# Products with V on four of the eight 64x32 tiles of TensorE, a head in two halves of 1024 queries with one accumulator bank

## The chip, the cores and the metric

The kernel runs on one core of a Trainium2 chip. A core has TensorE (matrix products; its results go to PSUM, eight banks of 128 partitions x 512 float32), VectorE, ScalarE and GpSimd for everything else, and DMA queues for transfers. The metric is the device time of one execution in microseconds (us). The profile names the engines PE (TensorE's products), PEld (its weight loads), DVE (VectorE), ACT (ScalarE), POOL (GpSimd) and SP (the queue that issues most transfers).

## The reference

Two multi-head attentions over the same x, mixed token by token with a gate (cut to what matters):

```python
x = A_x                                   # 1 x 2048 x 512, 32 heads of 16
g = sigmoid((x * gate_w).sum(-1, keepdims=True))
# for each of A and B, with its own wqkv and wo:
qkv = (x @ wqkv).reshape(B, S, 3, H, Dh)  # q, k, v
scores = einsum("bhqd,bhkd->bhqk", q, k) * Dh ** -0.5
p = softmax(scores, axis=-1)
o = einsum("bhqk,bhkd->bhqd", p, v)
a_or_b = o.reshape(B, S, D) @ wo
return g * a + (1 - g) * b
```

All data is float32. So there are 64 heads in all, each with 2048 x 2048 scores.

## The kernel before

**Stages.** A prologue splits the inputs into high and low parts, computes q, k and v for all heads (products of 128x128 weights with 512 columns, L298 and L351) and stores them to memory. Then one long loop runs over 1024 *rounds*: a round is one tile of 128 keys of one head, 16 rounds to a head. Finished heads are stored unnormalised with their denominators (17 rows: 16 of the head and one of sums), and read back, normalised and multiplied with wo some heads later (`project_out`, L564): side 0 after head 31, in four groups of four output tiles, side 1 after head 55, the last group in the tail.

**A round.** TensorE is used as eight independent tiles of 64 rows x 32 columns: two row halves (rows 0 to 63 and 64 to 127, `HALVES`) times four column groups. Three kinds of work run on them:

- *Scores* (`score`, L218): for 128 keys and 512 queries, four products of 50 rows x 32 columns, on the four tiles of one row half; the two halves take turns (`rows()`). One PSUM bank `ps_st` per 512 queries. ScalarE turns it into exponentials (L220, the letter `e`), which go to a buffer `p` of 2048 queries.
- *Maxima* for a head that comes 22 rounds later (`max_plain`, L153, letter `m`): the same shape with queries as rows, into a bank `ps_m`, reduced by VectorE (L159). One bank of each two rounds goes another way: ScalarE first writes a relu of a small difference product (`max_rise`, L166, letter `D`, bank `ps_st`), and VectorE reduces bank and relu together (`max_pair`, L171, letter `A`).
- *Products with V* (`attend`, L697): for each 128 queries ("a quarter" of 512) the 128 keys as two halves of 64, each on its own row half and into its own accumulator bank (`acc[0]`, `acc[1]`); the four chunks of 512 queries lie on the four column groups. All eight tiles work on it. The operands are float32.

**The order** is written out by hand. For two rounds it is one of two equal strings

```python
FULL = "Dmemme3eem2emmeeAe3", "Dmemme3eem2emmeeAe3"
```

where a digit issues that many quarters for all four chunks. Each engine takes its instructions in this order. The products with V run two rounds behind the exponentials. PSUM: three banks `ps_m`, three `ps_st`, two accumulators.

**End of a head** (L716 to L723): ScalarE copies both accumulators to SBUF (L720, two copies), GpSimd adds them (L722), and a transfer stores the head (`od`). The first product with V of the next head must wait for these copies, since it overwrites the accumulators. Before it come six banks of scores in the order (`D m e m m e`).

**The last 22 rounds** have no more maxima to compute: the order is `LATE`, and all six free banks take scores in turn (`ring`, `result_bank`). The last head runs its queries in four blocks of 512, so that its outputs can be normalised and projected one block at a time (`tail`, `add_parts`, `token_gates`).

**In the prologue** the v projections (`project_v`, L351, one `ps_st` bank each) alternate with `run_ahead`: after every second one, six banks of scores for the maxima of the first heads, of which every second lies in a `ps_st` bank too (`early`).

## Time and profile before

| what | us |
|---|---|
| median of 3 runs (lowest, highest) | 2723.86 (2723.26, 2723.9) |
| the profiled execution's own time | 2724.57 |
| its span | 2722.8 |
| busy PE / PEld / DVE / ACT / POOL | 2577.0 / 1521.8 / 2361.3 / 2401.3 / 355.4 |
| granted TensorE clock, mean | 0.999 |

The page of the profile gives, for each group of instructions, the line of the kernel, the engine, the operation, output and inputs with their shapes, how many there were, the busy time, the mean length in nanoseconds of one record, and the idle time of the engine just ahead of them with what ended it. Records of one engine overlap, because its pipeline takes the next instruction before the last has ended; so the mean length of one is longer than the time from one to the next. A float32 product with V has two records (the page lists 32320 for about 16160 instructions). The rows by window give each engine's busy time and, in brackets, its number of instructions.

### The profile page before, as it was taken

How to read it: one execution, taken by the hardware profiler on the slowest of the kernel's cores; microseconds unless marked ns; L12 is line 12 of the kernel's file. 1: busy time of each engine (PE TensorE's matmuls, PEld its weight loads, DVE VectorE, ACT ScalarE, POOL GpSimd, SP SyncE). 2: the span in 40 equal slices, each digit the busy share in tenths (PEclk: the TensorE clock that was granted, in tenths of full speed). 3: DMA queues.
4: the chain of work that ended last, by engine and by line, in shares of the span. 5: the costliest groups of instructions: out<-in, count | busy, mean ns of one | idle time of the engine just before them, and what ended most of it. 6: DMA issues, size and time to landing. Idle time of an engine off the chain costs nothing.

```text
span 2722.8 us, 147771 instructions
## 1 busy us (share of the span) xinstructions
PE 2577.0 (95%) x66710; PEld 1521.8 (56%) x66710; DVE 2361.3 (87%) x4474; ACT 2401.3 (88%) x4862; POOL 355.4 (13%) x594
## 2 busy tenths in 40 slices
PE   9999999999999999999999999999999999999998
PEld 7777555555555555555555565555555555555553
DVE  5444799999999999999999978899999999998884
ACT  4222699999999999999999968899999999998796
POOL 2010022220000000000100323000100011012212
PEclk9999999999999999999999999999999999999999
DMA  5342212111111111111211322111111111112102
GB/s 199 113 159 99 71 47 66 54 51 39 51 38 32 34 42 51 38 40 39 62 36 34 100 61 75 35 33 33 54 38 39 40 58 46 32 57 84 44 25 96
DMA packets 95934, 159.62 MB, mean 59 GB/s; under 512 B 26182, under 2 KB 43974, under 8 KB 95302
## 3 DMA queue, kind: packets, MB, share of 16 engines
q1 hardware_dynamic: 91590, 139.68, 16.4%
q8 instruction: 522, 8.55, 1.4%
q0 software_dynamic: 2560, 8.91, 1.3%
q10 hardware_dynamic: 1152, 1.57, 0.2%
q14 instruction: 110, 0.90, 0.1%
HBM read 100.56 MB, written 49.54 MB: 55 GB/s over the span
## 4 chain that ended last, share of the span: by engine, by line
PE 73%; ACT 17%; DVE 7%; issue 2%; DMA 1%; SPq 0%; DVEq 0%; ACTq 0%
PE acc L697 30%; PE ps_st L218 20%; ACT p L220 15%; PE ps_m L153 9%; PE ps_st L298 6%; DVE mxp L159 6%; PE ps_st L351 3%; PE ps_m L564 3%; ACT ev L720 2%; PE ps_st L153 1%; DVE rise L171 1%; DMA x_st<-xd 0%; DVE rn L520 0%; DMA raw<-in_xT 0%; PE ps_st L564 0%
## 5 line engine op out<-in xcount | busy, mean ns | idle before, releaser
L220 ACT ACTIVATE p<-ps_st 128x512 f32<-128x512 f32 x4044 | 2105.1, 725 | 82.3 <-PE ps_st L218 77.8
L159 DVE TENSOR_REDUCE mxp<-ps_m 128x1 f32<-128x512 f32 x3048 | 1893.0, 682 | 160.5 <-PE ps_m L153 64.8
L218 PE MATMUL ps_st<-q_st,k_st 50*32 50x512 f16 x16192 | 1516.7, 382 | 82.8 <-ACT p L220 0.5
L697 PE MATMUL acc<-p,vg 64*17 64x384 f32 (+1 forms) x32320 | 1367.6, 379 | 39.3 <-ACT ev L720 35.5
L153 PE MATMUL ps_m<-k_st,q_st 48*32 48x512 f16 x14192 | 1118.7, 380 | 1.7 <-DVE mxp L171 1.3
L218 PEld LDWEIGHTS <-k_st 50*32 50x32 f16 x16384 | 636.8, 89 | 834.4 <-issue 712.9
L697 PEld LDWEIGHTS acc<-p,vg 64*17 64x17 f32 x32320 | 553.7, 92 | 117.6 <-ACT ev L720 54.4
L153 PEld LDWEIGHTS <-q_st 48*32 48x32 f16 x16384 | 444.1, 89 | 145.8 <-issue 57.0
L166 ACT ACTIVATE rise<-ps_st 128x512 f32<-128x512 f32 x500 | 357.2, 715 | 0.0
L171 DVE CUSTOM_DVE_ANT_0 rise<-ps_m,rise 128x512 f32<-128x512 f32 x500 | 340.6, 681 | 0.0
L722 POOL TENSOR_TENSOR ev<-ev_lo,ev 128x512 f32<-128x512 f32 x63 | 80.4, 1277 | 1022.5 <-ACT ev L720 1022.5
L153 PE MATMUL ps_st<-x_st,q_st 48*32 48x512 f16 x2000 | 210.4, 377 | 0.0
L181 POOL TENSOR_SCALAR mrow<-mrow 128x16 f32<-128x16 f32 x64 | 16.4, 257 | 1018.5 <-DVE mrow L180 1018.5
L318 ACT ACTIVATE parts<-ps_st 128x512 f16<-128x512 f32 x64 | 38.0, 597 | 111.8 <-PE ps_st L298 105.1
L319 DVE SCALAR_TENSOR_TENSOR parts<-ps_st,parts 128x512 f16<-128x512 f32 x64 | 44.0, 691 | 95.8 <-ACT parts L318 89.7
L354 ACT COPY v_st<-ps_st 128x512 f32<-128x512 f32 x32 | 18.8, 587 | 98.9 <-PE ps_st L351 96.5
L564 PE MATMUL ps_m<-wo,ot 128*128 128x512 f32 x348 | 83.7, 395 | 2.2 <-DVE mxp L159 2.2
L564 PEld LDWEIGHTS ps_m<-wo,ot 128*128 128x128 f32 x348 | 64.7, 189 | 21.3 <-issue 5.5
L298 PE MATMUL ps_st<-xh,whi 128*128 128x512 f32 x224 | 59.9, 389 | 0.0
L298 PE MATMUL ps_st<-xh,wlo 128*128 128x512 f32 x224 | 59.9, 389 | 0.0
L298 PE MATMUL ps_st<-xl,whi 128*128 128x512 f32 x224 | 59.9, 389 | 0.0
L298 PEld LDWEIGHTS ps_st<-xh,wlo 128*128 128x128 f32 x224 | 42.0, 188 | 8.8
(120 smaller groups left out, 997.2 us busy)
## 6 DMA issues: line engine op xcount, KB each, us to landing
k_st<-kd SPq DMA_DIRECT2D x128, 128.0 KB
q_st<-qd SPq DMA_DIRECT2D x128, 128.0 KB
od<-ev SPq DMA_DIRECT2D x63, 256.0 KB
vd<-v_st SPq DMA_DIRECT2D x32, 272.0 KB
vg<-vd POOLq DMA_DIRECT2D x32, 272.0 KB, 4.2
qd<-parts SPq DMA_DIRECT2D x32, 256.0 KB
kd<-parts SPq DMA_DIRECT2D x32, 256.0 KB
k_st<-kd SPq DMA_DIRECT2D x128, 64.0 KB
```

The source lines that it names most:

```text
L153: pe.matmul(ps[j:j + 32], q[b:b + SC, t * P + j:t * P + j + 32], k, start=True, stop=True, tile_position=(b, j))
L159: dve.tensor_reduce(o[:, c:c + 1], ps, op=ALU.max, axis=AX.X)
L166: act.activation(rises[m], ps, AF.Relu)
L171: dve.tensor_tensor_reduce(out=rise, in0=ps, in1=rise, scale=1.0, scalar=LOWEST, op0=ALU.add, op1=ALU.max, accum_out=o[:, 0:1])
L218: pe.matmul(ps[j:j + 32], k[b:b + SC + 2, kk * P + j:kk * P + j + 32], q[b:b + SC + 2, cc * 512:(cc + 1) * 512], start=True, stop=True, ti ...
L220: act.activation(pt[r][:, c * 512:(c + 1) * 512], ps, AF.Exp, scale=SCALE / UNIT ** 2)
L298: pe.matmul(ps, w[a][:, k], (xh, xl)[b][cc][:, k], start=n == 0, stop=n == 3 * KC - 1)
L351: pe.matmul(ps, a[:, k, o:o + P], b[:, k], start=n == 0, stop=n == 3 * KC - 1)
L564: pe.matmul(ps, ot[a][:, slot, tt * P:(tt + 1) * P], wt[b][:, g], start=first and i == 0, stop=last and i == 2)
L697: pe.matmul(acc[i][32 * c:32 * c + 17, qa * P:qb * P], v[b:b + 64, 4 * a + c if final else kt, j], p[b:b + 64, c * 512 + qa * P:c * 512 + ...
L720: act.copy(parts[i], acc[i])
L722: pool.tensor_tensor(ev, parts[0], ev, op=ALU.add)
```

## The change

- **Tiles.** `tiles_of(0)` is rows 0 to 63 with columns 0 to 63 and rows 64 to 127 with columns 64 to 127; `tiles_of(1)` is the other four tiles. All products with V run on the first four. A bank of scores goes to whichever four have less work issued to them (`load`, one unit for a quarter or a bank), so mostly to the second. Every bank of scores is now written half from one row half and half from the other.
- **One accumulator.** The two key halves of a product now lie in different partitions of one bank: keys 0 to 63 in partitions 0 to 63 and keys 64 to 127 in partitions 64 to 127, for two chunks of 512 queries. So a bank holds 1024 queries, and a head runs in two halves: all 16 key tiles for queries 0 to 1023, then all for 1024 to 2047. A *unit* is one key tile and 1024 queries, two to a round. The freed bank goes to `ps_st` (four instead of three).
- **End of a half head.** One copy of the one bank: by VectorE for the first half (both halves of head 62 and the last head's first three blocks too), by ScalarE for the second; then the store. The two key halves are no longer added by GpSimd at once; they are stored apart and added when they are read back (`add_den`, `add_num`, on GpSimd, one add for the denominators of a group and one for each group and chunk). The stores, and the loads of numerators and denominators, are twice as many or more.
- **Order.** `FULL` covers four rounds; the quarters are spread as one or two at a time between the banks of scores. A digit issues quarters of one unit, four instructions each. The end of every half head falls on the end of the string, with six banks of scores (`m e A D e m`) between the last product with V of the old half and the first of the new one. The row work of VectorE is called at the letters `Q` and `R`.
- One `max_rise` moves from the end of the prologue into the loop.

At the end of a head, ScalarE's order changes. The names are the exponentials (`p<-ps_st`), the relu (`rise`) and the copies out of the accumulators; before:

```order
L166 ACTIVATE rise<-ps_st 128x512
L220 ACTIVATE p<-ps_st 128x512 x8
L720 COPY ev_lo<-acc_74 128x512
L720 COPY ev<-acc_75 128x512
L166 ACTIVATE rise<-ps_st 128x512
L220 ACTIVATE p<-ps_st 128x512 x8
```

and now, at the end of a second half:

```order
L165 ACTIVATE rise<-ps_st 128x512
L222 ACTIVATE p<-ps_st 128x512 x9
L743 COPY ev<-acc 128x512
L222 ACTIVATE p<-ps_st 128x512
L165 ACTIVATE rise<-ps_st 128x512
L222 ACTIVATE p<-ps_st 128x512 x6
```

Two copies for each head have become one; the exponentials and relus are as many as before.

The other copy is in VectorE's order, at the end of a first half, between the reductions (`mxp<-ps_m`; the two ISA rows are the one of L170):

```order
L158 TENSOR_REDUCE mxp<-ps_m 128x1 x6
L743 COPY ev<-acc 128x512
L158 TENSOR_REDUCE mxp<-ps_m 128x1
L170 ISA rise,mxp<-ps_m,rise 128x512
L170 ISA mxp 128x1
L179 TENSOR_REDUCE mrow<-mxp 128x16
```

where before there were only reductions at this point:

```order
L159 TENSOR_REDUCE mxp<-ps_m 128x1 x6
L171 ISA rise,mxp<-ps_m,rise 128x512
L171 ISA mxp 128x1
L159 TENSOR_REDUCE mxp<-ps_m 128x1 x3
L180 TENSOR_REDUCE mrow<-mxp 128x16
```

VectorE gets one more operation for each head.

The diff, cut to its core (what is left out are the layouts of the loads and stores, the last head's schedule and the end of the prologue):

```diff
-    ps_st = ctx.enter_context(tc.tile_pool(name="ps_st", bufs=3, space=PSUM))
+    ps_st = ctx.enter_context(tc.tile_pool(name="ps_st", bufs=4, space=PSUM))
...
-    acc = [ps_acc.tile([P, 512], F32, name=f"acc{i}") for i in range(2)]
+    acc = ps_acc.tile([P, 512], F32, name="acc")
...
+    load = [0, 0]
+
+    def tiles_of(i):
+        return [(HALVES[(j // 64 + i) % 2], j) for j in range(0, P, 32)]
+
+    def next_tiles():
+        i = int(load[0] >= load[1])
+        load[i] += 1
+        return tiles_of(i)
...
-        for j in range(0, P, 32):
-            pe.matmul(ps[j:j + 32], q[b:b + SC, t * P + j:t * P + j + 32], k, start=True, stop=True,
+        for b, j in next_tiles():
+            pe.matmul(ps[j:j + 32], q[b:b + SC, t * P + j:t * P + j + 32], k[b:b + SC], start=True, stop=True,
                       tile_position=(b, j))
...
-        for j in range(0, P, 32):
+        for b, j in next_tiles():
             pe.matmul(ps[j:j + 32], k[b:b + SC + 2, kk * P + j:kk * P + j + 32],
                       q[b:b + SC + 2, cc * 512:(cc + 1) * 512], start=True, stop=True, tile_position=(b, j))
...
+    def add_num(G, c):
+        pool.tensor_tensor(nums[G, c], nums[G, c], nums.pop(("p", G, c)), op=ALU.add)
...
+    def attend(u, qa, qb):
+        h, w = divmod(u, 2 * NT)
...
+        for i, (b, d) in enumerate(tiles_of(0)):
+            c = i % 2
+            pe.matmul(acc[d:d + 17, qa * P:qb * P], v[b:b + 64, 2 * (w % n) + c if h == NH - 1 else w % n, j],
+                      pt[u][b:b + 64, c * 512 + qa * P:c * 512 + qb * P], start=w % n == qa == 0,
+                      stop=w % n == n - 1, tile_position=(b, d), skip_group_check=True)
+        load[0] += qb - qa
...
-            parts = [work.tile([P, 512], F32, name=n) for n in ("ev_lo", "ev")]
-            for i in range(2):
-                act.copy(parts[i], acc[i])
-            ev = parts[1]
-            pool.tensor_tensor(ev, parts[0], ev, op=ALU.add)
-            nc.sync.dma_start(od[G][j].rearrange("c r t -> (c r) t"), ev)
+            ev = work.tile([P, 512], F32, name="ev")
+            (dve.tensor_copy if w < NT or h == NH - 2 else act.copy)(ev, acc)
+            nc.sync.dma_start(od[G][j, w // NT].rearrange("c r t -> (c r) t"), ev)
...
-    FULL = "Dmemme3eem2emmeeAe3", "Dmemme3eem2emmeeAe3"
-    EDGE = FULL
-    LATE = "ee4eeee4ee"
+    FULL = "QDQemQ2e1m1e2em1Qe1m2eQ1Dm1e2AQ1em1e3mem1e1Q2e1m1e1m1e1m1e1RQ2mReA"
+    LATE = "e2" * 8
...
                 for a in projects:
                     project_out(*a)
+                    load[:] = [0, 0]
                 projects.clear()
```

## The prediction

> **What bounds the kernel now.** I read the page's chain first, then busy time by window, then the groups and waits of the long loop, then the timeline at the places that the change touches. The chain alone misleads:

> ```profile
> PE 73%; ACT 17%; DVE 7%; issue 2%; DMA 1%; SPq 0%; DVEq 0%; ACTq 0%
> ```

> PE's records carry a modelled, pipelined end, so they nearly always touch. The windows (busy PE, PEld, DVE, ACT, POOL; instructions in brackets) say more. They are the prologue, the loop, the side 0 projections, the loop, the side 1 projections and the last head:

> ```profile
> 60.00:310.00 250.00, 239.54 (x1512) 180.38 (x1515) 108.14 (x171) 62.41 (x109) 25.16 (x28) 1.00 0.34 117
> 600.00:1500.00 900.00, 852.81 (x25422) 482.08 (x25414) 862.98 (x1660) 899.54 (x1836) 69.53 (x153) 1.00 0.15 41
> 1515.00:1707.00 192.00, 182.87 (x4552) 110.91 (x4552) 160.25 (x300) 157.62 (x322) 60.44 (x75) 1.00 0.23 72
> 1720.00:1912.00 192.00, 182.05 (x5420) 102.92 (x5419) 183.94 (x354) 191.91 (x392) 10.04 (x25) 1.00 0.13 38
> 2395.00:2585.00 190.00, 180.81 (x4742) 107.25 (x4728) 166.53 (x316) 163.57 (x334) 40.34 (x53) 1.00 0.20 62
> 2667.00:2705.00 38.00, 34.93 (x485) 13.29 (x486) 16.34 (x33) 30.96 (x63) 13.43 (x18) 0.96 0.21 75
> ```

> In the loop ACT is busy 899.54 of 900 us with 1836 instructions: 0.490 us each, end to end. A head is 64 exponentials, 8 relus and 2 copies, 74 x 0.490 = 36.26 us. DVE is busy 95.9%, idle 37 us in 24.8 heads, 1.49 us a head. The groups (whole run), and the loop's waits:

> ```profile
> L220 ACT ACTIVATE p<-ps_st 128x512 f32<-128x512 f32 x4044 | 2105.1, 725 | 82.3 <-PE ps_st L218 77.8 <-PE ps_m L218 3.5
> L218 PE MATMUL ps_st<-q_st,k_st 50*32 50x512 f16 x16192 | 1516.7, 382 | 82.8 <-ACT p L220 0.5 <-ACT v_st L354 0.2
> L697 PE MATMUL acc<-p,vg 64*17 64x384 f32 x15968 | 1004.7, 484 | 35.5 <-ACT ev L720 35.5
> L697 PE MATMUL acc<-p,vg 64*17 64x128 f32 x15968 | 332.9, 269 | 0.0
> L579 DVE TENSOR_SCALAR o_acc<-ps_m,gate 128x512 f32<-128x512 f32 x16 | 12.0, 751 | 31.5 <-PE ps_m L564 31.5
> L520 DVE RECIPROCAL rn<-dn 128x32 f32<-128x32 f32 x28 | 9.7, 345 | 0.0
> ```
> ```profile
> PEld L218 <- issue: 276.1, 870, 0.5
> PEld acc L697 <- ACT ev L720: 20.9, 24, 0.9
> ```

> PE's weight loads for the scores stand still 276.1 us in these 900: PE is ahead and waits for a bank that ACT has not read. So ACT is the bound in the loop, DVE is next, and PE has about 30% to spare. In the projection windows ACT is busy only 82% and 86%: PE starves it.

> **The copies: the term that should be certain.** The end of one head, in the timeline (start, length, what):

> ```profile
> 631.25 0.64 ACT L720 COPY ev_lo<-acc 128x512 f32<-128x512 f32 x1
> 631.72 0.67 ACT L720 COPY ev<-acc 128x512 f32<-128x512 f32 x1
> 632.20 0.69 ACT L166 ACTIVATE rise<-ps_st 128x512 f32<-128x512 f32 x1
> 632.44 0.87 PE L697 MATMUL acc<-p,vg 64*17 64x384 f32 x16 [0.57 <-ACT ev L720]
> ```

> From one copy to the next is 0.48 us. Heads 0 to 61 lose one of two: 62 x 0.48 = **-29.8**. Head 62 loses both: **-1.0**.

> The copy on DVE has no row before. Below, it costs a reduction of the same 512 columns, 0.60 from one to the next (below, at 283); above, the 0.751 of L579, which writes 512 columns from PSUM. I take 0.60. It hides in DVE's 1.49 us of idle time, which falls to 1.49 - 0.60 - 0.48 = 0.41 a head. That cover is thin; without it, what exceeds 0.41 comes back on the path (second rival). Queued behind the copy on DVE are one to three reductions, and PE waits for their banks; ACT meanwhile has e, D, e, 3 x 0.49 = 1.5 us, besides what is queued.

> PE now waits at the accumulator twice a head instead of once (20.9/24 = 0.87 us). Below: one copy less, 0.4 each. Above: a copy behind three reductions, 4 x 0.60 = 2.4. Either is covered by 276.1/24.8 = 11 us of waiting for ACT. Cost 0.

> **PE's own work.** From 128 to 384 columns a record grows by 215 ns, so 128 columns take 107 ns in each of two records, 0.215 us a quarter; the rest, 0.16, is pipeline. A score bank is 382 - 162 = 220 ns. Before, a tile has 64 quarters and 64 banks a head: 13.8 + 14.1 = 27.9 us of 36.26. Now one four have 128 quarters, 27.5 us, and the other four up to 128 banks, 28.2, of 35.78. The sum is unchanged; cost 0. Pieces of 128 columns already run at full rate:

> ```profile
> 1001.24 0.66 PE L697 MATMUL acc<-p,vg 64*17 64x128 f32 x32
> ```

> 32 records on eight tiles, four deep: (0.66 - 0.16)/4 = 0.125 us each, the stagger of eight starts included.

> **The fourth `ps_st` bank, in the prologue.** One pair of v projections with its six score banks:

> ```profile
> 282.74 0.40 PE L153 MATMUL ps_st<-k_st,q_st 48*32 48x512 f16 x4
> 283.01 0.68 DVE L159 TENSOR_REDUCE mxp<-ps_st 128x1 f32<-128x512 f32 x1
> 283.61 0.68 DVE L159 TENSOR_REDUCE mxp<-ps_m 128x1 f32<-128x512 f32 x1
> 283.75 0.76 PEld L351 LDWEIGHTS ps_st<-wvhi,xh 128*128 128x128 f32 x4 [0.91 <-DVE mxp L159]
> 283.75 1.20 PE L351 MATMUL ps_st<-wvhi,xh 128*128 128x512 f32 x4 [0.61 <-DVE mxp L159]
> ```

> A pair takes five `ps_st` banks: projection, three of the six scores, projection. With three, the second projection needs the bank of the first such score and waits for its reduction, the second one (283.01 + 0.68 = 283.69; it starts at 283.75). With four it takes the first projection's bank, which ACT has emptied. In the prologue's waits:

> ```profile
> PEld ps_st L351 <- DVE mxp L159: 14.4, 16, 0.9
> PE ps_st L351 <- DVE mxp L159: 9.7, 16, 0.7
> ```

> PE bounds this stage (239.54 of 250), DVE works only 108, so nothing is late next. Bounds -9.7 (products) and -14.4 (weight loads); the product's record ends 0.16 after its tile is free, which makes up most of the difference: **-14.4**.

> **Projections.** Eight times (four for each side) PE runs several output tiles in a row and ACT starves:

> ```profile
> 1562.78 11.14 PE L564 MATMUL ps_m<-wo,ot 128*128 128x512 f32 x48 [0.28 <-DVE mxp L159]
> 1573.85 0.86 PE L697 MATMUL acc<-p,vg 64*17 64x384 f32 x16
> 1574.51 0.42 PE L218 MATMUL ps_st<-q_st,k_st 50*32 50x512 f16 x8
> 1574.96 2.56 ACT L220 ACTIVATE p<-ps_st 128x512 f32<-128x512 f32 x5 [11.44 <-PE ps_st L218]
> ```

> The first exponential's scores wait 0.66 us behind products with V that hold all eight tiles. Now these hold four; the scores wait for one bank of maxima, 0.22: -0.44. A fourth bank lets ACT work up to 0.49 longer into the burst: 0 to -0.49. Per burst -0.4 to -0.9, times 8 = -3.5 to -7.4. PE is far ahead there, so the fourth bank is full: **-7.3**. GpSimd's adds (16 a side, about 1.3 us each) fit beside its 60 of 192 us.

> **Losses.** At each of seven group ends DVE makes four reciprocals of 0.345 us, 1.4 us. They hid in 1.49 a head; now in 0.41: 0 to 1.0 each; **+3** of 0 to 7.

> In the last 22 rounds ACT needs 8 x 0.49 = 3.92 us for two rounds. PE needed 8 x 0.215 + 4 x 0.22 = 2.6; now the first four tiles alone need 16 x 0.215 = 3.4. The output projections of the last head, some 9 us on all tiles, had 8 x 1.3 = 10.7 us to fit into and now have 8 x 0.5 = 3.9: up to +5, though ACT already loses 38 - 30.96 = 7 us there. The last products with V run on four tiles, 8 x 0.215 = +1.7. Against it, on the chain at the end

> ```profile
> 2708.46 0.54 issue
> 2709.00 0.68 DVE o_num L551
> 2709.68 0.61 DVE ev L708
> 2710.32 0.63 ACT ev_hi L710
> ```

> ACT now makes `ev_hi` straight from the accumulator, which takes out the add (0.61) and some of what it waited for: about -1.3. Together -2 to +7: **+3**.

> More stores and loads (window share of DMA 0.15) and GpSimd's loss of 63 adds of 1.3 us lie off the path. The store now waits for one copy, not copy and add, so what is behind it on SP (the next head's loads) is not later.

> **Sum.** 2724.6 (the profiled execution, 1.8 over its span) - 29.8 - 1.0 - 14.4 - 7.3 + 3 + 3 = 2678; the median of the runs lies 0.7 below that execution: **2677 us**, 1.7% faster.

> **The rivals.**

> *DVE takes over (chance 0.13).* If the copy and the hitch of PE waiting behind it cost 0.5 us a head more than DVE's 0.41, ACT's gain is gone: the head stays 36.3, and the prologue and the projections remain: 2724 - 14 - 7 + 3 = 2706. For it: 98.9% busy. Against: the 1.49 is the records' figure, in which every pause hides 0.08 (681 ns a record, 600 from one to the next); the true slack is larger.

> *PE becomes the bound (0.09, slower).* Its place is the chain of quarters on the first four tiles: 128 a head must each take less than 36.26/128 = 0.283 us to be faster than before, against 0.215. If each of the two passes showed 40 ns more, because a four-tile queue hides the weight load (92 ns a record) less than eight did, a quarter would take 0.295, a head 37.8, and the time 2724 + 62 x 1.5 - 14 = 2803. Against: the 0.125 us of the 32-record row.

> *The two row halves exclude each other in a bank (0.02, slower).* Before, each score bank and each accumulator was written from one row half. Now all are written from both. If these took turns, a quarter would take 0.43, a head 55 us, the time about 3900. [...]

> **Chances and range.** Forecast 0.74, rivals 0.13, 0.09, 0.02, the rest small shifts. Its own range: all losses at their worst and the smaller gains, 2724 - 31 - 10 - 3.5 + 7 + 7 = 2694; the other way, 2724 - 31 - 14 - 7 - 2, with up to 8 more if the smoother order ends small waits, 2662. The DVE rival widens it: 2660 to 2708. What can be told from no change here is 0.2%, 5 us. Faster 0.87, same 0.03, slower 0.10.

> **What would show it.** Right: in the loop ACT still above 99% with 73 instructions a head, heads of 35.8 us; no L351 wait for DVE; ACT's pauses at the bursts near 10.5 instead of 11.44; DVE near 98%. Wrong: waits of ACT for `ps_st` in the loop, PE's 276 us of waiting gone, or the products with V longer than 0.215 us a quarter.

## The result, and the profile after

The changed kernel takes 2854.61 us (median of 4 runs, 2852.75 to 2859.02), the kernel before 2723.65 on the same chip: ratio 1.0483, 95% interval 1.0465 to 1.0501. It is **slower by 131 us** where 47 us less were predicted. The profiled execution took 2855.93, its span is 2854.1.

The windows of the changed kernel, to be held against those of the kernel before (busy PE, PEld, DVE, ACT, POOL):

```profile
60.00:310.00 250.00, 247.02 (x2092) 190.36 (x2091) 122.51 (x198) 77.47 (x139) 25.98 (x32) 1.00 0.35 122
600.00:1500.00 900.00, 806.02 (x30189) 579.93 (x30172) 837.49 (x1601) 864.47 (x1723) 40.77 (x131) 1.00 0.16 47
1515.00:1707.00 192.00, 168.53 (x5391) 122.65 (x5378) 153.46 (x289) 151.49 (x303) 55.98 (x66) 0.97 0.27 89
1720.00:1912.00 192.00, 178.85 (x5729) 126.31 (x5717) 162.42 (x311) 159.80 (x322) 20.27 (x37) 0.99 0.15 44
```

In the loop ACT is busy 96.1% instead of 99.9%, and DVE less than before too. PE is *less* busy (806 of 900 us, before 853) although it got through *more* instructions: 30189 + 30172 in 900 us, 67.0 a microsecond, where before 25422 + 25414 were 56.5. So nothing on DVE, ACT or PE's array is full. The waits of the same 900 us say who stands still:

```profile
PEld L152 <- issue: 93.2, 251, 1.8
PEld acc L720 <- issue: 86.8, 124, 1.5
PE acc L720 <- issue: 46.5, 93, 1.2
PEld L220 <- issue: 38.6, 90, 1.2
DVE mxp L158 <- PE ps_m L152: 36.9, 91, 1.1
ACT p L222 <- PE ps_st L220: 24.3, 63, 1.1
```

"issue" is time in which the engine waited for nothing that the profile shows. Before, such a pause of PE lasted at most 0.5 us and stood at the scores and the maxima (`PEld L218`, and 19.8 us at L153), where the prediction read it as PE waiting for a bank. Now it lasts up to 1.8 us and stands in front of products with V as well, and DVE and ACT wait for PE. The chain of waits has 9% "issue" where it had 2%:

```profile
PE 68%; DVE 14%; issue 9%; ACT 5%; DMA 3%; SPq 1%; POOL 0%; ACTq 0%; DVEq 0%; POOLq 0%
```

In the timeline the pauses come at a beat. Three neighbours (start, length, what, and the idle time ahead of it):

```profile
1000.14 0.29 PE L720 MATMUL acc<-p,vg 64*17 64x128 f32 x3 [0.70 <-issue]
1003.88 0.29 PE L720 MATMUL acc<-p,vg 64*17 64x128 f32 x3 [0.31 <-issue]
1007.63 0.40 PE L720 MATMUL acc<-p,vg 64*17 64x128 f32 x4 [0.47 <-issue]
```

They are 3.74 and 3.75 us apart. In the records of these 900 us, 242 of PE's instructions (weight loads included) start over 0.35 us after the one before, and half of these lie exactly 256 instructions apart (123 of 241 spacings; in `v_128`, a run told of below, 171 of 207). The page's first row and its list of DMA queues give the reason away; of the changed kernel:

```profile
PE 2589.7 (91%) x83094; PEld 1856.0 (65%) x83094; DVE 2405.9 (84%) x4538; ACT 2414.3 (85%) x4794; POOL 325.3 (11%) x583
q8 instruction: 650, 10.65, 1.6%
```

and of the kernel before:

```profile
q8 instruction: 522, 8.55, 1.4%
```

10.65 MB in 650 packets are 16384 bytes each. They are 64 bytes for each of the 2 x 83094 PE instructions, and the same division gives 64 before (2 x 66710). So q8 carries PE's instructions, 256 to a packet. This gives a theory, called F below: **PE is fed its instructions in blocks of 256, and no faster than one block in about 3.75 us.** A head of the changed kernel has 2560 of them: `FULL` has 24 pieces of V for four rounds, 96 a head, each four instructions on each of four tiles, 1536, and the 128 banks of scores and maxima have 8 each, 1024. (The trace has 2558 a head. The expectations below say 2608, which is a miscount.) That is ten blocks, 37.5 us at 3.75, and the heads took 38.3. A head before had 2048, 8 blocks, 30 us, which fitted into ACT's 36.26.

Where the 131 us lie, by the ends of every 64th exponential on ACT (us; the three right columns are runs that are told of below):

| stretch | before | after | v_512 | v_512_add | v_512_add_dve |
|---|---|---|---|---|---|
| to the first exponential of the loop's head 0 | 287.9 | 273.8 | 274.0 | 272.6 | 273.9 |
| head 0 | 49.5 | 48.9 | 46.2 | 46.2 | 46.2 |
| heads 1 to 32 | 1161.7 | 1225.7 | 1159.9 | 1159.9 | 1149.4 |
| heads 33 to 37 (projections, side 0) | 227.7 | 253.4 | 253.0 | 226.6 | 225.2 |
| heads 38 to 56 | 689.5 | 721.6 | 688.0 | 688.0 | 682.3 |
| heads 57 to 61 (projections, side 1) | 213.7 | 234.7 | 218.1 | 212.5 | 210.6 |
| heads 62 and 63 | 74.8 | 75.8 | 77.6 | 74.3 | 77.4 |
| behind the last exponential | 17.9 | 20.1 | 20.2 | 20.2 | 20.2 |
| span | 2722.8 | 2854.1 | 2737.1 | 2700.2 | 2685.1 |

The prologue's gain is there. Of the other stretches head 0 is 0.6 us shorter than before, and all the rest are longer.

### The profile page after: what moved, and what is told of

Read it like the earlier page. It is cut to its first block, busy times and chain, and to the rows that moved or that the text cites. A ratio compares the mean times of both kernels' runs of the same rounds, so it can differ in the third digit from the quotient of the medians.

```text
span 2854.1 us, 181748 instructions
## 1 busy us (share of the span) xinstructions
PE 2589.7 (91%) x83094; PEld 1856.0 (65%) x83094; DVE 2405.9 (84%) x4538; ACT 2414.3 (85%) x4794; POOL 325.3 (11%) x583
## 3 DMA queue, kind: packets, MB, share of 16 engines
q8 instruction: 650, 10.65, 1.6%
q0 software_dynamic: 2560, 8.91, 1.1%
## 4 chain that ended last, share of the span: by engine, by line
PE 68%; DVE 14%; issue 9%; ACT 5%; DMA 3%; SPq 1%; POOL 0%; ACTq 0%; DVEq 0%; POOLq 0%
PE acc L720 30%; PE ps_st L220 13%; PE ps_m L152 12%; DVE mxp L158 10%; PE ps_st L300 6%; ACT p L222 4%; PE ps_st L353 3%; PE ps_m L587 3%; DVE rise L170 2%; PE ps_st L152 2%; DMA o_part<-od 1%; DVE ev L743 1%; ACT ev L743 1%; ACT rise L165 1%; DMA q_st<-qd 0%
## 5 line engine op out<-in xcount | busy, mean ns | idle before, releaser
L222 ACT ACTIVATE p<-ps_st 128x512 f32<-128x512 f32 x4051 | 2146.5, 675 | 208.7 <-PE ps_m L152 104.5
L720 PE MATMUL acc<-p,vg 64*17 64x128 f32 (+2 forms) x48672 | 2066.3, 308 | 157.7 <-issue 139.9
L158 DVE TENSOR_REDUCE mxp<-ps_m 128x1 f32<-128x512 f32 x3048 | 1920.8, 682 | 208.0 <-PE ps_m L152 130.6
L220 PE MATMUL ps_st<-q_st,k_st 50*32 50x512 f16 x16220 | 1640.6, 381 | 46.8 <-issue 36.0
L720 PEld LDWEIGHTS acc<-p,vg 64*17 64x17 f32 x48672 | 1325.1, 93 | 385.0 <-issue 238.0
L152 PE MATMUL ps_m<-k_st,q_st 48*32 48x512 f16 x14192 | 1486.4, 381 | 42.7 <-issue 30.2
L152 PEld LDWEIGHTS <-q_st 48*32 48x32 f16 x16384 | 584.1, 90 | 317.0 <-issue 212.3
L220 PEld LDWEIGHTS <-k_st 50*32 50x32 f16 x16384 | 582.7, 90 | 205.9 <-issue 129.5
L170 DVE CUSTOM_DVE_ANT_0 rise<-ps_m,rise 128x512 f32<-128x512 f32 x500 | 341.6, 683 | 29.9 <-PE ps_m L152 14.3
L165 ACT ACTIVATE rise<-ps_st 128x512 f32<-128x512 f32 x500 | 337.0, 674 | 5.6 <-PE ps_st L152 4.8
L152 PE MATMUL ps_st<-x_st,q_st 48*32 48x512 f16 x2000 | 210.6, 380 | 4.0 <-issue 2.7
L180 POOL TENSOR_SCALAR mrow<-mrow 128x16 f32<-128x16 f32 x64 | 16.5, 257 | 1724.9 <-DVE mrow L179 1724.9
L559 POOL TENSOR_TENSOR o_num<-o_num,o_part 128x512 f32<-128x512 f32 x32 | 40.8, 1276 | 234.2 <-DMA o_part<-od 234.2
```

Source lines behind the costliest of these rows:

```text
L152: pe.matmul(ps[j:j + 32], q[b:b + SC, t * P + j:t * P + j + 32], k[b:b + SC], start=True, stop=True, tile_position=(b, j))
L158: dve.tensor_reduce(o[:, c:c + 1], ps, op=ALU.max, axis=AX.X)
L165: act.activation(rises[m], ps, AF.Relu)
L170: dve.tensor_tensor_reduce(out=rise, in0=ps, in1=rise, scale=1.0, scalar=LOWEST, op0=ALU.add, op1=ALU.max, accum_out=o[:, 0:1])
L220: pe.matmul(ps[j:j + 32], k[b:b + SC + 2, kk * P + j:kk * P + j + 32], q[b:b + SC + 2, cc * 512:(cc + 1) * 512], start=True, stop=True, ti ...
L222: act.activation(pt[u][:, c * 512:(c + 1) * 512], ps, AF.Exp, scale=SCALE / UNIT ** 2)
```

## The experiments

### The number of instructions, and nothing else

F says that the count alone matters, whatever tiles, banks or copies. Two kernels have the same count, 3072 a head, and share little else: `v_128` is the changed kernel with its products with V cut into four pieces of 128 columns at eight places of the order, and `before_128` is the kernel *before* with its products cut the same way.

```diff
 # before_128, in attend
-        for c in range(NQ):
-            for i in (turn[0], 1 - turn[0]):
...
-                pe.matmul(acc[i][32 * c:32 * c + 17, qa * P:qb * P], v[b:b + 64, 4 * a + c if final else kt, j],
+        for qp in range(qa, qb):
+            for c in range(NQ):
+                for i in (turn[0], 1 - turn[0]):
...
+                    pe.matmul(acc[i][32 * c:32 * c + 17, qp * P:qp * P + P], v[b:b + 64, 4 * a + c if final else kt, j],
```

`v_512` and `v_256` go the other way. The order issues whole units of 512 columns, in one piece (1536 instructions a head) or in two (2048):

```diff
 # v_512; v_256 and v_128 have this order too, and a loop over pieces in attend
-    FULL = "QDQemQ2e1m1e2em1Qe1m2eQ1Dm1e2AQ1em1e3mem1e1Q2e1m1e1m1e1m1e1RQ2mReA"
+    FULL = "QDQemQ4eme4emQem4eQDme4AQeme4meme4Qem4emem4eRQmReA"
```

> The same order again, each unit cut into four pieces of 128 columns issued one right after the other: 3072 instructions a head. F: 12 x 3.75 = 45 us a head, 2680 + 61 x 9.2 = about 3240. T: the columns are the same, near 2855 or little more. D: near 2855.

> The kernel before with one edit: its products with V are issued in pieces of 128 columns where it had 384, at the same places of the order, on all eight tiles and with both accumulators: 3072 instructions a head instead of 2048. F: 45 us a head instead of 36.3, 2724 + 61 x 8.7 = about 3250. T: the eight tiles run pieces of 128 at full rate (0.215 us a quarter), so within 1% of 2724. D: 2724.

> The changed kernel, its products with V issued as whole units of 512 queries (one 512-column instruction on each of the four tiles) at the first place of each unit in the order, instead of in pieces of mostly 128 columns. The same columns on the same tiles, a third of the instructions for V: with two weight loads and two products each, PE has 1536 instructions a head instead of 2608 (before: 2048). Theory F (PE cannot be fed with more than 256 instructions in about 3.75 us, so 2608 take 38.2 us a head): PE is no longer the bound, ACT is again, 73 x 0.490 = 35.8 us a head, the whole near 2680 us. Theory T (a quarter on four tiles costs the array more, about 0.30 us instead of 0.215): unchanged, near 2855. Theory D (VectorE with its copy is the bound): unchanged, near 2855.

> The same order as in the run with whole units, each unit cut into two pieces of 256 columns issued one right after the other: 2048 instructions a head, as many as the kernel before had. F: 2048/256 x 3.75 = 30 us, below ACT's 35.8: still near 2680. T and D: near 2855.

Measured, in one execution each: `v_128` 3314.65, `before_128` 3315.59: the same time to 0.03% from two different kernels, 45.7 us a head in both (heads 1 to 32). The kernel before, with its eight tiles and two accumulators, loses 590 us by the cut alone. F holds; a block took a little longer than it said (45.7 / 12 = 3.81 us), so both came out some 70 us above their forecasts. The loop of `before_128` starves like the changed kernel's:

```profile
600.00:1500.00 900.00, 733.81 (x30330) 501.45 (x30336) 709.11 (x1323) 747.18 (x1462) 59.85 (x133) 0.99 0.12 34
```

30330 + 30336 instructions in 900 us, again 67 a microsecond, with no engine busy for more than 748.

`v_512` came to 2737.23 (ratio 1.0027, 1.0010 to 1.0043) and `v_256` to 2739.54 (1.0047, 1.0029 to 1.0066). The 117 us between the changed kernel and `v_512` are gone, and 512 more instructions a head cost nothing as long as they fit. But 2737 is not the 2677 of the sum: 60 us are lost elsewhere.

### A ceiling, or a price for each short piece?

Two more runs put the count elsewhere. `s_256` leaves V whole and makes each bank of *scores* in two pieces of 256 columns (2560 a head). `v_2304` takes two and three pieces of V in turn (2304).

```diff
 # s_256, in score (and the same in scores_bank, outside the prologue)
-        for b, j in next_tiles():
-            pe.matmul(ps[j:j + 32], k[b:b + SC + 2, kk * P + j:kk * P + j + 32],
-                      q[b:b + SC + 2, cc * 512:(cc + 1) * 512], start=True, stop=True, tile_position=(b, j))
+        tiles = next_tiles()
+        for p in (0,) if u < 4 else (0, 256):
+            n = 512 if u < 4 else 256
+            for b, j in tiles:
+                pe.matmul(ps[j:j + 32, p:p + n], k[b:b + SC + 2, kk * P + j:kk * P + j + 32],
+                          q[b:b + SC + 2, cc * 512 + p:cc * 512 + p + n], start=True, stop=True,
 # v_2304, against v_256, in attend
-        for p0, p1 in zip((0, 2), (2, 4)):
+        for p0, p1 in (((0, 2), (2, 4)), ((0, 2), (2, 3), (3, 4)))[u % 2]:
```

> The run with whole 512-column products with V, with each bank of scores in the loop made by two pieces of 256 columns on the same four tiles (16 instructions on PE a bank where there were 8); the products with V stay whole. PE then gets about 2560 instructions a head where v_512 has 1536 and the changed kernel 2608, with no more columns through the array. Theory F (PE is fed its instructions in blocks of 256 at one block per about 3.75 us): a head takes 2560 / 256 x 3.75 = 37.5 us (37.2 to 38.0) with PE idle for no one, about 80 us more in all, 2805 to 2840. Rival S (short pieces of the product with V, at fp32, are what is slow, by their weight loads or their accumulation): scores in half pieces cost no more than whole ones, heads stay at 36.15 and the whole at 2737 to 2745.

> The run with whole 512-column products with V, with every other unit of 512 columns in two pieces of 256 and the others in three of 256, 128 and 128: 2304 instructions on PE a head, between v_256 (2048) and the changed kernel (2608). Theory F, now with a number: in the five runs that ask for more, PE's queue q8 brought 208 to 212 blocks in 800 us whatever was asked for, and 177 in those with 2048. 2304 a head ask for 9 blocks in 36.15 us, 199 in 800 us, below that ceiling: heads stay at 36.15 to 36.4 us, the whole within 2735 to 2755, and q8 shows 196 to 199 blocks between 700 and 1500 us. Rival C (a cost in proportion, so much for every short piece): the loss of the changed kernel over v_256, 115 us for 560 instructions a head, is shared out, and 2304 loses 256 / 560 of it, 2790 to 2795.

Measured, again in one execution each: `s_256` 2872.57, heads of 38.6 us; `v_2304` 2745.31, plain heads of 36.18. V was whole in the one that lost, and in short pieces in the one that did not: it is not the short float32 pieces. Nor is it a price for each piece: with 512 instructions in place of its 560, rival C gives `v_2304` 2797. (`s_256` was 33 us beyond F's range: its blocks came at 3.86 us, not 3.75.) The queue's packets between 700 and 1500 us show the ceiling best; of `v_2304`, then of the changed kernel, then of `before_128`:

```profile
q8 instruction: 197, 3.23, 1.7%
```
```profile
q8 instruction: 209, 3.42, 1.9%
```
```profile
q8 instruction: 211, 3.46, 1.8%
```

| kernel | instructions a head | blocks in 800 us at 36.15 us a head | blocks that came | us a head, heads 1 to 32 |
|---|---|---|---|---|
| v_512 | 1536 | 133 | 132 | 36.25 |
| before / v_256 | 2048 | 177 | 177 / 176 | 36.30 / 36.26 |
| v_2304 | 2304 | 199 | 197 | 36.30 |
| s_256 | 2560 | 221 | 208 | 38.58 |
| changed kernel | 2560 | 221 | 209 | 38.30 |
| v_128 / before_128 | 3072 | 266 | 211 / 211 | 45.71 / 45.68 |

Up to 199 the blocks come as they are asked for; above, with 221 to 266 asked for, 208 to 211 come. It is a ceiling, one block in about 3.8 us, 67 instructions a microsecond. It is not a fixed time for each instruction: between 700 and 1500 us of the changed kernel the fastest 128 instructions in a row start within 1.1 us, 116 a microsecond, but the fastest 1024 need 13.6 us, 75 a microsecond. (Half of PE's instructions are weight loads in every run, in the changed kernel 83094 of 166188, so their count alone fits as well as that of all; the packets of 256, the pauses 256 apart and these bursts are what speaks for the queue.) A float32 product costs four of them (two weight loads, two products: a full head of the changed kernel has 768 records of each at L720, for the 384 products in its order), so four quarters in single pieces cost 16 where one of 512 columns costs 4.

### The other 60 us: the projections

In `v_512` the heads 33 to 37 take 25 us more than before. Its waits between 1521 and 1685 us (three projections):

```profile
POOL o_num L559 <- DMA o_part<-od: 77.0, 12, 20.6
ACT p L222 <- PE ps_st L220: 55.0, 3, 18.9
PE ps_m L587 <- DVE mxp L158: 14.6, 3, 5.6
DVE mt L187 <- POOL mparts L182: 13.8, 3, 5.3
```

Read from the bottom: DVE stands at the transposition of the next head's maxima (L187) for POOL (L182); behind it in DVE's order are the reductions that PE's projection waits for; PE holds up ACT, 18.9 us instead of 11.44. And POOL stands for the second partial sum. The timeline of POOL there:

```profile
1535.00 1.28 POOL L559 TENSOR_TENSOR o_num<-o_num,o_part 128x512 f32<-128x512 f32 x1 [16.64 <-DMA o_part<-od]
1549.94 1.26 POOL L559 TENSOR_TENSOR o_num<-o_num,o_part 128x512 f32<-128x512 f32 x1 [2.45 <-DMA o_part<-od]
1551.16 0.26 POOL L180 TENSOR_SCALAR mrow<-mrow 128x16 f32<-128x16 f32 x1
1551.77 0.22 POOL L182 TENSOR_TENSOR mparts<-mrow,mparts 128x16 f16<-128x16 f32 x1
```

The four additions end at 1551.2; the maxima, 0.7 us of work, stood behind them. Two edits:

```diff
 # v_512_op4: more buffers, so that the loads need not wait for the additions
-        nums["p", G, c] = work.tile([P, 512], F32, name="o_part")
+        nums["p", G, c] = work.tile([P, 512], F32, name="o_part", bufs=4)
 # v_512_add: that, and the additions later in the order
-                at(end + 23 + 16 * c + i, add_num, G, c)
-                at(end + 26 + 16 * c + 2 * i, normalize, G, c)
+                at(end + 28 + 16 * c + i, add_num, G, c)
+                at(end + 28 + 16 * c + 2 * i, normalize, G, c)
```

> The run with whole 512-column products with V, and four buffers for the second partial sum (o_part) where there were two; nothing else. In v_512's trace the heads with projections (34 to 36) took 54.3 to 55.3 us where before's took 47.8, and DVE stood 5.3 us at each of three projections for POOL's maxima (L182), which stood behind POOL's additions of partial sums (L559), which waited for DMA o_part. Theory Q (the queue): with two buffers SP can't issue the third load before POOL's first addition, so loads and additions go one after the other, and POOL's maxima, DVE's transposition and PE's projection stand behind them. With four buffers the loads are issued at once, heads 34 to 36 go back to about 47.8, DVE's wait for L182 is under 1 us, and the whole is about 26 us shorter on side A and 4 on side B: 2705 to 2715 us. Theory B (bytes): twice the partial sums take twice the transfer, whoever holds them; the landing stays late, heads 34 to 36 stay at 53 to 55, and the whole stays within 2730 to 2737.

> The run with whole 512-column products with V, with four o_part buffers, and POOL's additions of the two partial sums put four to five rounds later, and the first two normalizations two and none (the loads stay where they were), so that POOL works off a head's row maxima (L180 to L182) before it waits for a partial sum. With four buffers alone (v_512_op4) the loads were issued at once and the heads with projections still took 54.9 to 57.4 us: 768 KB a group go at some 155 GB/s, and POOL, in order, holds the maxima behind the addition that waits for them. Theory P (POOL's order): DVE no longer waits for L182 and PE not for DVE there, heads 34 to 36 go to 47.5 to 49, and the whole is 20 to 28 us shorter than v_512: 2709 to 2717. Rival B (the bytes themselves): the landing is late for the projection as well, so heads 34 to 36 stay above 53 and PE waits for POOL's ot (L577, L580) or o_num instead, the whole within 2730 to 2740.

`v_512_op4` came to 2736.44 (1.0019, 0.9999 to 1.0040): heads 33 to 37 take 256 us. The loads were issued closer together, and the last addition could still begin only 21.0 us after the first issue (21.2 in `v_512`); theory Q (buffers) fell, the transfers take that long. `v_512_add` came to **2704.26**, ratio 0.9891 (0.9876 to 0.9906), 5 us below theory P's range: heads 34 to 36 take 47.5 us. POOL's row maxima now go first, and the sums have landed when it comes to them:

```profile
1538.64 0.22 POOL L182 TENSOR_TENSOR mparts<-mrow,mparts 128x16 f16<-128x16 f32 x1
1538.82 1.28 POOL L559 TENSOR_TENSOR o_num<-o_num,o_part 128x512 f32<-128x512 f32 x1
```

It was the place in POOL's order. Of the 36.8 us between the two spans, 26.4 and 5.6 lie in the heads with projections and 3.3 in the last two heads.

### The changed kernel with the same edit

> The changed kernel itself, in its own order of single quarters, with the one edit of v_512_add: four o_part buffers and POOL's additions of the partial sums four to five rounds later. Theory P+F (two separate losses): its heads with projections, 43.2, 54.0, 51.7, 54.4 and 50.2 us (heads 33 to 37), lose what POOL's wait adds and keep what PE's feeding adds: about 38, 50, 50, 50, 50, some 15 to 25 us less, the whole 2830 to 2842. Rival G (given back): PE is fed so late there that POOL's wait is hidden behind it; under 8 us come back, 2847 to 2856.

> The changed kernel itself, unaltered, on the same chip as the run after it here, since after_add (2812) was timed on another chip than the changed kernel (2855) and its plain heads, which the edit doesn't touch, were shorter too. If the chip or the execution sets PE's feeding rate: 2812 to 2840 here. If the edit does: 2850 to 2858.

> The changed kernel with POOL's additions of the partial sums later and four o_part buffers, once more, beside the changed kernel on the same chip. By the heads with projections alone (11 us less in the two traces) the edit brings 8 to 20 us here; by the whole difference of the first comparison 43 us.

`after_add` came to 2811.84 (ratio 1.0309, 1.0283 to 1.0335), but 30 of the 43 us lay in plain heads (heads 1 to 32 and 38 to 56: 16.4 and 13.5), which the edit doesn't touch, and it ran on another chip than the changed kernel had. Side by side on one chip the changed kernel took 2852.84 (`after_2`, 1.0477, 1.0450 to 1.0504) and the edited one 2847.36 (`after_add_2`, 1.0452, 1.0418 to 1.0485). The intervals overlap; heads 33 to 37 went from 258.1 to 249.6. So in the changed kernel itself the edit is worth some 5 us, not clearly told from none, less than the 8 us and the 43 us that were expected of it. The two losses don't add up: in the heads with projections on side 0 DVE stands 17.3 us for POOL's maxima (L182) in `v_512` and 4.5 in the changed kernel, where PE is late anyway. And the 43 us of the first comparison are not the edit's: the edited kernel alone differs by 35.5 us between the two chips, although `after_2` fell in the range that its expectation gave for the edit as the cause. The chip or the execution moves the ceiling by a little (212 blocks in 800 us in `after_add`, 208 to 210 in the three others); which of the two was not tried.

### The last 22 us: 0.38 us in each plain head

A plain head of `v_512` takes 36.15 us where 73 instructions of 0.490 us on ACT are 35.77. Its loop and its waits at the accumulator:

```profile
600.00:1500.00 900.00, 892.67 (x19095) 395.00 (x19080) 871.21 (x1686) 897.15 (x1816) 39.63 (x126) 1.00 0.17 50
```
```profile
PEld acc L720 <- DVE ev L743: 12.0, 24, 0.5
PEld acc L720 <- ACT ev L743: 3.4, 21, 0.3
```

Once a head PE stands 0.50 us for DVE's copy. In the 8 us behind that copy three exponentials end 0.67, 0.60 and 0.59 us after the one before instead of 0.49: the 0.38 us. Is it the single bank, the place of the copy, or DVE's lack of room?

```diff
 # v_512_acc2 (and v_512_acc2_op4 with the buffers above): two accumulators in turn, three ps_st banks
-    ps_st = ctx.enter_context(tc.tile_pool(name="ps_st", bufs=4, space=PSUM))
+    ps_st = ctx.enter_context(tc.tile_pool(name="ps_st", bufs=3, space=PSUM))
-    acc = ps_acc.tile([P, 512], F32, name="acc")
+    accs = [ps_acc.tile([P, 512], F32, name=f"acc{i}") for i in range(2)]
...
 # v_512_gap (and v_512_gap_add): first product later, last one earlier
-    FULL = "QDQemQ4eme4emQem4eQDme4AQeme4meme4Qem4emem4eRQmReA"
+    FULL = "QDQemQem4e4emQem4eQDme4AQeme4meme4Qem4em4emeRQmReA"
 # v_512_add_swap: last product ahead of one bank of maxima
+    FULL = "QDQemQ4eme4emQem4eQDme4AQeme4meme4Qem4eme4meRQmReA"
 # v_512_act: both copies on ACT
-            (dve.tensor_copy if w < NT or h == NH - 2 else act.copy)(ev, acc)
+            (dve.tensor_copy if h == NH - 2 else act.copy)(ev, acc)
 # v_512_add_dve: both on DVE
+            dve.tensor_copy(ev, acc)
```

> The run with whole 512-column products with V, and two accumulator banks taken in turn by the halves of a head, with three ps_st banks as before the change; still four tiles, halves and two copies a head. In v_512 a plain head took 36.15 us where its 73 ACT instructions at 0.490 are 35.77. Theory A (the accumulator): the 0.38 us are lost where PE stands up to 0.5 us at the single bank for DVE's copy, since PE has no slack left there; with two banks a plain head is 35.8 us, about 21 us less over the loop. The prologue loses its fourth bank and gives back about 14. Sum 2737 - 21 + 14 = 2730 (2725 to 2735). Theory N (not the accumulator: PE's array or DVE sets 36.15): heads stay at 36.15, and the whole is 2737 + 14 = 2751. In both the first loop exp ends near 288 us as in the kernel before (274 in v_512).

> Both edits, two accumulator banks and four buffers for o_part, on the run with whole 512-column products with V. If theories A and Q both hold, the two terms add up: 2737 - 21 + 14 - 30 = 2700 (2693 to 2708), faster than the kernel before by about 24 us, which is the 62 copies of 0.48 us that the change was costed at, minus what side effects remain. If only Q holds about 2721; if only A holds about 2730; if neither 2751.

> The run with whole 512-column products with V, with the first product of each four rounds two banks of scores later and the last one two banks earlier, so that DVE's copy of the single accumulator bank gets about 0.9 us more between a half's last product and the next half's first. In v_512 PE stood 0.50 us a head at that copy, and a plain head took 36.15 us where 73 ACT instructions of 0.490 are 35.77. Theory A (the stall at the single bank is where the 0.38 us go): PE's wait for DVE's copy goes to nearly 0 and a plain head takes 35.8 us, the whole 57 x 0.35 = 20 us less: 2715 to 2720. Theory N (DVE or PE's array has no room, the wait is only where it shows): the wait moves elsewhere, heads stay within 36.05 to 36.2, the whole within 2730 to 2740.

> Both edits, the later additions on POOL and the wider gap at the accumulator, on the run with whole 512-column products with V. If theories P and A both hold: 2737 - 25 - 20 = 2692 (2685 to 2700), about 30 us under the kernel before; if only P holds 2712, if only A 2717, if neither 2737.

> The run with whole 512-column products with V, with both copies of a head's accumulator on ACT (DVE copies only head 62). ACT then has 74 instructions a head, 36.26 us at 0.490, as before the change. Theory A (PE and then ACT stand for DVE's late copy): ACT takes its copy right behind an exponential, the stalls go with DVE's copy, a head takes 36.3 us, and the whole is 2740 to 2746, 0.1 us a head over v_512. Theory N (the stalls are not DVE's copy's): they stay and the instruction comes on top, 36.6 us a head, 2763 to 2770.

> v_512_add with the last product of each four rounds ahead of the maximum bank that stood before it, so that DVE finds its copy of the accumulator one reduction (0.60 us) earlier; the first product of the next four rounds stays where it was. In v_512 PE stood 0.50 us a head for that copy. Theory A (the copy's place behind a reduction on DVE costs the 0.38 us): a plain head goes from 36.15 to 35.8 us, the whole to 2680 to 2690. Theory O (the order is so tight that any bank moved takes ACT's next bank with it, as in v_512_gap, 36.96 us): heads stay at 36.15 or more, the whole at 2704 to 2750.

> v_512_add with both copies of a head on DVE, so that ACT has 72 instructions a head (35.28 us at 0.490) and DVE one more copy of 0.60 us. Theory D (DVE has no room left: 871 of 900 us busy in v_512): PE stands for two late copies a head, each gives back about 0.38 us, so a head takes 36.05 us and the whole 2698 to 2704, no more than 0.1 us a head from 36.15; if DVE becomes the bound itself a head takes 36.2 to 36.5 and the whole 2708 to 2725. Theory R (the stall is a matter of one place): 35.7 us, the whole 2675 to 2685.

| run | us (median) | ratio, 95% | a plain head, us |
|---|---|---|---|
| v_512_acc2 | 2830.90 | 1.0372 (1.0344 to 1.0400) | 37.53 |
| v_512_acc2_op4 | 2828.09 | 1.0363 (1.0331 to 1.0395) | 37.54 |
| v_512_gap | 2776.16 | 1.0156 (1.0141 to 1.0171) | 36.96 |
| v_512_gap_add | 2754.80 | 1.0075 (1.0058 to 1.0092) | 36.97 |
| v_512_act | 2741.29 | 1.0029 (1.0011 to 1.0047) | 36.26 |
| v_512_add_swap | 2705.39 | 0.9915 (0.9893 to 0.9938) | 36.17 |
| v_512_add_dve | 2686.40 | 0.9849 (0.9821 to 0.9877) | 35.84 |

`v_512_acc2` and the run with both edits missed both theories. With three `ps_st` banks ACT waits for scores 74 times in these 900 us, three times a head, so it says nothing on the accumulator, and much on the fourth bank: 1.4 us a head in this order, if the second accumulator by itself costs nothing.

```profile
ACT p L223 <- PE ps_st L221: 18.2, 74, 0.3
PE ps_st L221 <- ACT p L223: 14.0, 25, 0.6
```

`v_512_act` is the clean one: 74 x 0.490 = 36.26, measured 36.26. Without DVE's copy the stalls are gone to the last hundredth. But making room around the copy gave nothing. In `v_512_gap` (and `v_512_gap_add`) PE's wait for DVE's copy is gone and a head is 0.8 us longer, against both theories: other waits of PE came, for ACT's and DVE's banks. In `v_512_add_swap` it is gone too, and in its place stands, as often as there are heads,

```profile
PE ps_m L152 <- DVE mxp L158: 8.7, 24, 0.4
```

DVE's 0.60 us come either ahead of the accumulator or ahead of a bank of maxima, and PE, in order, waits for the one or the other. Theory A's mechanism (the single bank) fell; what stands is that a copy on DVE passes 0.38 us of its 0.60 on to ACT. `v_512_add_dve` agrees: 72 x 0.490 = 35.28, so two copies cost 0.56 there, and PE's wait is there twice a head,

```profile
600.00:1500.00 900.00, 888.48 (x19247) 402.52 (x19236) 886.73 (x1724) 894.76 (x1805) 44.38 (x131) 1.00 0.17 52
```
```profile
PEld acc L720 <- DVE ev L743: 25.1, 50, 0.5
```

yet each copy taken from ACT (0.49) is worth more than what DVE gives back. At 98.5% DVE is not the bound. This kernel came out between the two theories, 1.4 us above R's range, at **2686.4 us** (2684.9 to 2690.46), 1.5% under the kernel before and the shortest of all. Whether some order loses nothing at the copies stays open.

## Why the prediction was wrong

**PE's own work: the step that failed.** "The sum is unchanged; cost 0" counted the time that columns take in the array, tile by tile, and that was right: a quarter's record takes 270 ns, 256 columns 378, 384 columns 483, so 0.107 us for each 128 as before. What it left out is that PE must be *given* its instructions. The support for it was a burst, 32 records of 128 columns in 0.66 us. A short burst can run faster than the queue (128 instructions in 1.1 us, above); what a loop could keep up here is 67 instructions a microsecond. The instructions a head went from 2048 (the windows give it: 25422 + 25414 in 24.8 heads) to 2560, which the new order string gives. Price: 117 us, the whole difference between the changed kernel and `v_512`. The forecast missed by 178 us; of the other 60, as `v_512` and the runs from it show them, 37 are POOL's order and 22 the copy on DVE.

**The copies, -29.8.** 73 instructions a head and 0.490 us each are right, and in the changed kernel none of it arrives, since ACT waits for PE. In `v_512` 0.11 us a head arrive, since DVE's copy gives back 0.38.

**The copy on DVE.** 0.60 us is right (681 ns a record, 0.60 from one to the next). "It hides in DVE's 1.49 us of idle time" is wrong: an idle time summed over a head is no gap at the place where the copy falls. Mis-sized by 0.38 us a head, 22 us over the plain heads, seen in `v_512` and not separately in the changed kernel. This is the DVE rival's mechanism; its price there was 0.5.

**PE's wait at the accumulator.** 0.4 to 2.4 us were foreseen, 0.50 and 0.16 came. In `v_512` the cover of 11 us a head did not cover it: PE's pauses lie elsewhere in the head.

**The prologue, -14.4.** Measured -14.1. PE's wait for DVE at the v projections, 14.4 us before, in the changed kernel:

```profile
PEld ps_st L353 <- ACT v_st L356: 6.9, 16, 0.4
PEld ps_st L353 <- DVE mxp L158: 0.8, 2, 0.4
```

The fourth bank is the cause: `v_512_acc2`, with three, needs 288.1 us to the first exponential of the loop, as the kernel before did (287.9). But the listed waits of these weight loads for ACT and DVE fell only from 15.7 to 7.7 us, so that the number came out to 0.3 us was partly luck.

**The projections, -7.3.** Measured +25.7 for side 0 and +21.0 for side 1. "GpSimd's adds fit beside its 60 of 192 us" summed durations where the order decides: an addition that waits for its transfer (up to 20.6 us in `v_512`) holds what is queued behind it. In `v_512` that is the cause and worth 32 us over both sides; in the changed kernel feeding and this wait overlap, and the edit gives back some 5. The gain that was forecast came out small: `v_512_add`, with the wait gone, has 47.5 us a head against 47.8, -1.1 for side 0 and -1.2 for side 1.

**Group ends and tail, +3 each.** The tail is +3.2 in the changed kernel (75.8 + 20.1 against 74.8 + 17.9). A group end costs 0.38 us in `v_512` (36.53 against 36.15), 0.24 before (36.31 and 36.45): +1 in all, too small to matter.

**The rivals.** That PE becomes the bound was right as a direction and wrong as a mechanism: it priced a quarter on four tiles at 0.295 us, and a quarter stayed at 0.215. That its 2803 lay near the 2855 is luck. That row halves exclude each other in a bank, at a chance that was the author's estimate, fell: every bank of scores and of products with V is written from both, and `v_512` has heads of 36.15 us where this rival gave 55; in the changed kernel a record of 128 columns takes 270 ns, before 269.

## What to carry to other kernels

Count PE's instructions in a stretch, weight loads included, and hold them against what its instruction queue brought (here one block of 256 in about 3.8 us): when products were cut into shorter pieces here, the array's time stayed (0.107 us for each 128 columns) and the count grew (1536, 2048, 2560, 3072 a head). A pause of PE that the profile calls "issue", that is longer than the usual one (up to 1.8 us here, before at most 0.5) and comes every 256 instructions, was that queue here. An engine's idle time, summed over a loop, hid little here (in `v_512` 0.38 of the copy's 0.60 us came through, against 1.49 of idle time a head): look at what stands behind the new instruction, or behind the transfer it waits for, in that engine's own order.
